# A linear-attention and SwiGLU kernel: earlier DMA transposes and loads, dummy matmuls in the opening, and other PSUM banks for the early state

## The chip, the cores and the metric

The kernel runs on one core of a Trainium2 chip. The metric is device microseconds (us) from the first to the last instruction of one execution, plus about 1.8 us of overhead. Each run carries a state: slow when it is over 1.5% above the fastest run of its kernel, else fast. The medians given are over all runs.

TensorE (PE) does matrix products, VectorE (DVE), ScalarE (ACT) and GpSimd (POOL) do elementwise work, SyncE (SP) issues DMAs. GpSimd also issues DMAs here: all loads that convert float32 to bfloat16 (k and q but for the first block, the weights) and, from block 4 on, the loads of v. PSUM is the memory, in banks, that the matrix products are written to. PEld in the views is TensorE's weight load.

## The reference, cut to what matters

Decayed linear attention over 4 batches x 8 heads x 768 tokens x 64, in blocks with a running state, followed by a SwiGLU feed-forward network (FFN).

```python
for b in range(nb):                                   # per block
    intra = (q_b @ k_b.T * Dmask) @ v_b
    inter = (q_b * lam_pow) @ kv_state
    out_b = intra + inter
    kv_state = lam_block * kv_state + (k_b * rev_pow).T @ v_b
x = out.transpose(0, 2, 1, 3).reshape(3072, 512)      # tokens x 512
y = (silu(x @ w_gate) * (x @ w_val)) @ w_out          # 512 -> 1536 -> 512
```

The kernel uses blocks of 128 tokens, so there are N = 24 blocks (6 per batch, NB = 6).

## The kernel before

The program order is written by hand, and each engine executes its instructions in that order. A block n passes four stages: `load` (DMA), `transposes` (k and q need their head dimension on the partitions), `scores` (k times q) and `cluster` (output and state). Blocks 0 to 7 are transposed on TensorE. From block 8 on (`PE_T = 8`) SyncE issues a DMA transpose instead.

```python
    PE_T = 8
    TILES = [(0, 4), (4, 2), (6, 2)] + [(i, 4) for i in range(8, N, 4)]   # first block, blocks per FFN tile
    ld = ctx.enter_context(tc.tile_pool(name="ld", bufs=7))               # loaded k and q
    vpool = ctx.enter_context(tc.tile_pool(name="vpool", bufs=7))         # loaded v
    ...
    def transposes(n):
        t = apool.tile([128, 2, HP, BLK], BF16, name="qkT", tag="qkT", bufs=4)
        if n >= PE_T:
            nc.sync.dma_start_transpose(out=..., in_=...)     # kq_nat -> qkT
        else:
            ...                                               # 8 TensorE transposes, copied out by ACT and DVE
    def scores(n):
        sp = ps_s.tile([128, 2, HP, BLK], FP32, name="sp", tag="sp")
        ...  nc.tensor.matmul(sp[:, h2, p, :], kT[n][r, p, :], qT[n][r, p, :], start=True, stop=True)
    def cluster(n, scores_of=None):
        ...  # op = kv_bd x qT      (L221, needs the state)
        if scores_of is not None:
            scores(scores_of)                                 # L207, needs qkT of the NEXT block
        ...  # op += v_s x ssb (L227); x = op; up = k x v (L240); new state kv_st, kv_bd
```

After an opening (blocks 0 to 7 and the first two FFN tiles), the main loop makes one step per block. A step is three FFN groups (`ffn_fc`, gate and value products, L273), one attention block, and one output product (`ffn_out`, L297) whose store is issued on SyncE:

```python
            for pos in range(3):
                ffn_fc(tt, 3 * per + pos)
                if pos == 0:
                    ...
                    if n + 1 < N:
                        scale_v(n + 1)                # GpSimd
                        transposes(n + 1)             # SyncE: DMA transpose
                elif pos == 1:
                    cluster(n, n + 1 if n + 1 < N else None)
                elif pos == 2:
                    if n + 4 < N:
                        load(n + 4)                   # GpSimd: k, q, v
                    ffn_out(*outs.pop(0))             # ends with a store on SyncE
```

`keep_warm(times)` issues dummy 128x512 matmuls, whose result nobody reads.

## Time and profile before

| | before |
|---|---|
| median time, us | 295.75 (4 runs, 293.63 to 300.65) |
| profiled span, us | 294.3 |
| TensorE busy, us | 242.5 |
| TensorE idle in waits for DMA transposes, us | 39.6 in 14 waits |

From the page of the kernel before: the totals, then rows over 40 equal slices of the span. A digit is tenths busy (9 is 90% or more); PEclk is the granted TensorE clock, the share of full speed that the chip allows at that time, in tenths.

```profile
span 294.3 us, 4235 instructions
...
PE 242.5 (82%) x1677; PEld 128.1 (44%) x1677; DVE 104.9 (36%) x168; ACT 79.3 (27%) x152; POOL 112.6 (38%) x150
...
PE   8689996999095839958599696896688999999994
...
PEclk9859996899759859999689997999979999999998
DMA  9999999990918792277491879254902200000122
```

TensorE has holes all through the middle of the run, and the granted clock dips with them. No engine is full there. Only the DMA row is full, and only in the first nine slices (up to about 66 us). TensorE is 90% busy or more in five of these nine slices, so what bounds the opening can't be read from these rows; in the middle it is no engine.

The list of waits names the cause (engine, line, waited for; us in total, times, longest):

```profile
PE sp L207 <- DMA qkT<-kq_nat: 39.6, 14, 7.6
```

Two stretches of the timeline show how one such wait comes about (start, us, engine, line, operation; in brackets the idle time before it and what ended it):

```profile
123.72 0.33 SPq L301 DMA_DIRECT2D out_dram<-osb  x1
124.22 1.46 SPq L184 DMA_TRANSPOSE qkT<-kq_nat  x1
...
126.36 0.39 PE L221 MATMUL op<-qkT,kv_bd 128*128 128x128 bf16 x4
...
129.75 0.40 PE L207 MATMUL sp<-qkT 64*128 64x128 bf16 x8 [3.00 <-DMA qkT<-kq_nat]
...
143.40 0.61 PE L207 MATMUL sp<-qkT 64*128 64x128 bf16 x8 [4.68 <-DMA qkT<-kq_nat]
...
144.72 1.89 PE L273 MATMUL gp<-xT,wg 128*128 128x512 bf16 x4
```

The transpose is issued right behind the store of the output before it, at 124.22. TensorE wants the result about 2.5 us later, at about 126.7, and gets it at 129.75. After a wait of 3.00 us the scores still run at full rate (0.40 us for eight). After 4.68 us they take 0.61, and four gate matmuls take 1.89 us where 1.03 is usual. That agrees with the Trainium skill, "TensorE: Matmul & The Clock Gate", Part 1, which says that the array clock falls to half after an idle window of about 3.4 us.

How long a transpose takes depends on what else moves. From the chain of waits (start, us, what):

```profile
73.32 8.29 DMA qkT<-kq_nat
...
114.69 3.05 DMA qkT<-kq_nat
```

```profile
71.90 0.95 POOL L84 DMA_DIRECT2D kq_nat<-in_k_dram  x1
72.85 0.88 POOL L85 DMA_DIRECT2D kq_nat<-in_q_dram  x1
73.71 0.91 POOL L79 DMA_DIRECT2D v_raw<-in_v_dram  x1
```

The transpose of 8.29 us runs beside the three loads of a block. Around the one of 3.05 us GpSimd issued no load: it did nothing between 110 and 120 us.

### The profile page before, as it was taken

To read this page: it belongs to the slowest core of one execution; us is meant where nothing else is said; L and a number is where in the kernel's file an instruction comes from. 1 tells how busy PE (TensorE), PEld (TensorE's weight loads), DVE (VectorE), ACT (ScalarE), POOL (GpSimd) and SP (SyncE) were. 2 spreads that over 40 slices of the span, in tenths; PEclk is the share of its full clock that TensorE was granted. 3 is DMA by queue.
4 is the path that set the end of the run, shared out by engine and by line. 5 is a ranking of instruction groups with operands and counts; after the bars stand their busy time and mean duration, and the time that the engine had idled before them with its cause. 6 is when DMAs were issued, how large, how long until landed. Compare 5 with 4: busy or idle time off the path is not lost.

```text
span 294.3 us, 4235 instructions
## 1 busy us (share of the span) xinstructions
PE 242.5 (82%) x1677; PEld 128.1 (44%) x1677; DVE 104.9 (36%) x168; ACT 79.3 (27%) x152; POOL 112.6 (38%) x150
## 2 busy tenths in 40 slices
PE   8689996999095839958599696896688999999994
PEld 3455454877054523433244342443244444444441
DVE  3744452566032322442214333334134242222200
ACT  6635433462001202212021130230203223232321
POOL 6796699714242820607154282062430310000000
PEclk9859996899759859999689997999979999999998
DMA  9999999990918792277491879254902200000122
GB/s 130 197 150 193 215 219 201 209 104 0 141 10 137 97 119 71 19 126 95 47 133 19 135 102 115 71 66 79 136 7 75 71 36 2 36 36 36 38 94 84
DMA packets 83075, 28.32 MB, mean 96 GB/s; under 512 B 73072, under 2 KB 78704, under 8 KB 83056
## 3 DMA queue, kind: packets, MB, share of 16 engines
q0 software_dynamic: 56320, 16.00, 50.5%
q1 hardware_dynamic: 26736, 12.07, 18.7%
q8 instruction: 13, 0.21, 0.3%
q14 instruction: 6, 0.05, 0.1%
HBM read 28.32 MB, written 6.29 MB: 118 GB/s over the span
## 4 chain that ended last, share of the span: by engine, by line
PE 67%; DMA 25%; POOL 3%; DVE 1%; ACT 1%; issue 1%; SPq 0%; ACTq 0%; DVEq 0%; POOLq 0%
DMA qkT<-kq_nat 23%; PE yp L297 22%; PE gp L273 20%; PE vp L273 17%; PE op L227 3%; PE sp L207 3%; DMA v_raw<-in_v_dram 2%; POOL v_s L177 1%; PE up L240 1%; DVE ssb L213 1%; PE tp L193 1%; PE op L221 1%; ACT kv_bd L251 1%; POOL wg L103 1%; DVE h_sb L289 0%
## 5 line engine op out<-in xcount | busy, mean ns | idle before, releaser
L289 DVE TENSOR_TENSOR h_sb<-sil,vp 128x512 bf16<-128x512 bf16 (+1 forms) x84 | 51.1, 611 | 123.3 <-PE vp L273 110.2
L273 PE MATMUL gp<-xT,wg 128*128 128x512 bf16 (+3 forms) x344 | 82.3, 365 | 0.8 <-ACT xT L232 0.7
L273 PE MATMUL vp<-xT,wv 128*128 128x512 bf16 (+3 forms) x344 | 81.1, 361 | 0.0
L286 ACT ACTIVATE sil<-gp 128x512 bf16<-128x512 f32 (+1 forms) x84 | 44.7, 536 | 124.8 <-PE gp L273 124.7
L297 PE MATMUL yp<-wo,h_sb 128*128 128x512 bf16 x288 | 68.1, 390 | 0.0
L253 POOL CAST kv_bd<-kv_st 64x256 bf16<-64x256 f32 x26 | 10.3, 396 | 113.8 <-DVE kv_st L246 83.4
L273 PEld LDWEIGHTS <-wv 128*128 128x128 bf16 x344 | 35.1, 103 | 32.1 <-issue 3.4
L273 PEld LDWEIGHTS <-wg 128*128 128x128 bf16 x344 | 32.8, 102 | 30.3 <-issue 3.6
L297 PEld LDWEIGHTS <-h_sb 128*128 128x128 bf16 x288 | 29.3, 102 | 35.9 <-issue 4.3
L207 PE MATMUL sp<-qkT 64*128 64x128 bf16 x192 | 10.8, 240 | 40.2 <-DMA qkT<-kq_nat 39.6
L213 DVE TENSOR_TENSOR ssb<-sp,mask 128x1024 bf16<-128x1024 f32 (+1 forms) x28 | 29.6, 1068 | 39.3 <-PE sp L207 39.3
L300 ACT COPY osb<-yp 128x512 f32<-128x512 f32 x24 | 14.1, 586 | 69.7 <-PE yp L297 69.7
L177 POOL TENSOR_TENSOR v_s<-v_raw,rev 128x512 bf16<-128x512 f32 x24 | 25.8, 1075 | 5.7 <-DMA v_raw<-in_v_dram 3.1
L207 PEld LDWEIGHTS <-qkT 64*128 64x128 bf16 x192 | 6.3, 102 | 45.1 <-DMA qkT<-kq_nat 42.6
L84 POOL DMA_DIRECT2D kq_nat<-in_k_dram x23 | 21.6, 939 | 1.6 <-DMA wg<-in_moe_w_gate_dram 0.8
L85 POOL DMA_DIRECT2D kq_nat<-in_q_dram x23 | 20.4, 888 | 2.5 <-DMA wg<-in_moe_w_gate_dram 1.5
L79 POOL DMA_DIRECT2D v_raw<-in_v_dram x20 | 18.2, 911 | 0.7 <-DMA wv<-in_moe_w_val_dram 0.7
L227 PE MATMUL op<-ssb,v_s 128*64 128x128 bf16 x192 | 12.0, 258 | 2.4 <-POOL v_s L177 2.4
L234 DVE TENSOR_TENSOR xT<-op,qscale 128x512 bf16<-128x512 f32 x16 | 10.9, 681 | 0.0
L221 PE MATMUL op<-qkT,kv_bd 128*128 128x128 bf16 x80 | 8.5, 233 | 2.4 <-ACT kv_bd L251 2.4
L227 PEld LDWEIGHTS <-v_s 128*64 128x64 bf16 x192 | 7.4, 127 | 5.8 <-POOL v_s L177 3.1
L221 PEld LDWEIGHTS <-kv_bd 128*128 128x128 bf16 x80 | 6.4, 104 | 5.8 <-ACT kv_bd L251 2.8
(47 smaller groups left out, 89.5 us busy)
## 6 DMA issues: line engine op xcount, KB each, us to landing
out_dram<-osb SPq DMA_DIRECT2D x24, 256.0 KB, 2.2
v_raw<-in_v_dram POOLq DMA_DIRECT2D x20, 256.0 KB, 6.0
kq_nat<-in_k_dram POOLq DMA_DIRECT2D x23, 128.0 KB, 4.7
kq_nat<-in_q_dram POOLq DMA_DIRECT2D x23, 128.0 KB, 5.7
wo<-in_moe_w_out_dram POOLq DMA_DIRECT2D x4, 384.0 KB, 7.7
wg<-in_moe_w_gate_dram POOLq DMA_DIRECT2D x3, 384.0 KB, 8.0
wv<-in_moe_w_val_dram POOLq DMA_DIRECT2D x3, 384.0 KB, 9.2
v_raw<-in_v_dram SPq DMA_DIRECT2D x4, 256.0 KB, 6.7
```

Source lines behind the costliest of these rows:

```text
L79: eng.dma_start(out=v_raw[n], in_=v5[b, j])
L84: nc.gpsimd.dma_start(out=t[:, 0], in_=k5[b, j])
L85: nc.gpsimd.dma_start(out=t[:, 1], in_=q5[b, j])
L177: nc.gpsimd.tensor_tensor(out=t, in0=v_raw.pop(n), in1=bap(rev, [[1, H], [0, D]]), op=ALU.mult)
L207: nc.tensor.matmul(sp[:, h2, p, :], kT[n][r, p, :], qT[n][r, p, :], start=True, stop=True)
L213: nc.vector.tensor_tensor(out=s[:, :, ps], in0=sp[:, :, ps], in1=mask[:, :, ps], op=ALU.mult)
L221: nc.tensor.matmul(op[:, p, :], kv_bd[n % 2][:, p, :], qT[n][:, p, :], start=(p == 0), stop=False, skip_group_check=True)
L227: nc.tensor.matmul(op[64 * h2:64 * h2 + 64, p, :], v_s[n][:, 2 * p + h2, :], ssb[n][:, h2, p, :], start=(j == 0 and p == 0), stop=(p == HP ...
L273: nc.tensor.matmul(gv[tt, fc][i][:, lo:hi], w[c][:, mc, fs], xT[:, mc, t0 + lo:t0 + hi], start=(mc == 0), stop=(mc == MC - 1))
L286: nc.scalar.activation(sil[:, 0:nt], gv[tt, fc][0][:, 0:nt], AF.Silu)
L289: nc.vector.tensor_tensor(out=h_sb[tt][:, fc, 0:nt], in0=sil[:, 0:nt], in1=gv.pop((tt, fc))[1][:, 0:nt], op=ALU.mult)
L297: nc.tensor.matmul(op, h_sb[tt][:, fc, sub * 128:(sub + 1) * 128], wo_sb[c][:, f, :], start=(fc == 0), stop=(fc == FC - 1))
```

## The change

The intent: issue DMA transposes three blocks ahead and loads six ahead, so that a transpose has two more steps to land; keep the clock up in the opening with 19 more dummies; move cluster 5 in between FFN matmuls of the second tile; and let the state accumulators (`up`) of blocks 4 to 7 use the output PSUM banks, which are free then.

```diff
-    ld = ctx.enter_context(tc.tile_pool(name="ld", bufs=7))
-    vpool = ctx.enter_context(tc.tile_pool(name="vpool", bufs=7))
-    apool = ctx.enter_context(tc.tile_pool(name="apool", bufs=3))
+    ld = ctx.enter_context(tc.tile_pool(name="ld", bufs=10))
+    vpool = ctx.enter_context(tc.tile_pool(name="vpool", bufs=9))
+    apool = ctx.enter_context(tc.tile_pool(name="apool", bufs=4))
 ... load_kq(1) moved behind the causal mask; qkT bufs 4 -> 6
-            up = (ps_o if n < FIRST else ps_f).tile(...)
+            up = (ps_o if n < PE_T else ps_f).tile(...)
 ... opening:
     scores(0)
-    transposes(1)
     scale_v(1)
     load_w(0)
+    keep_warm(5)
     cluster(0)
+    transposes(1)
+    nc.scalar.activation(primed, lamb, AF.Silu)
+    keep_warm(2)
     scores(1)
 ... and so on for blocks 1 to 3: value scaling earlier, keep_warm(4), (1), (4), (3)
 ... end of the first tile and second tile:
-        elif fc == 10:
-            scale_v(5)
-            transposes(5)
-        elif fc == 11:
-            cluster(4, 5)
-            cluster(5)
+        elif fc == 9:
+            cluster(4)
+            transposes(5)
+        elif fc == 10:
+            scores(5)
+            load(8)
+    fc_mms(1, 0, 0, BLK)
+    cluster(5)
+    fc_mms(1, 1, 0, BLK)
+    ffn_fc(1, 0, BLK)
+    ffn_fc(1, 1, BLK)
 ... loads 9 to 13 and the DMA transposes 8 to 10 inside the second tile
 ... main loop:
                         scale_v(n + 1)
-                        transposes(n + 1)
+                    if n + 3 < N:
+                        transposes(n + 3)
-                    if n + 4 < N:
-                        load(n + 4)
+                    if n + 6 < N:
+                        load(n + 6)
```

## The prediction

> **What bounds the kernel now.** Span 294.3 us, TensorE busy 242.5. By the list of waits, TensorE stood idle 39.6 us in 14 waits of score matmuls for a DMA transpose (longest 7.6 us); the chain of waits puts 23% of the span on those transposes. The timeline shows why: each transpose is issued 3 to 4 us before its scores and takes 3.0 to 8.3 us to land. The longer waits cost twice: after them matmuls run at half rate for 3 to 4 us (four 512-wide gate matmuls take 1.82 us instead of 0.86), which agrees with the Trainium skill, "TensorE: Matmul & The Clock Gate", Part 1: the clock halves after an idle window of about 3.4 us. So the main loop is bound by transpose latency, not by an engine. In the opening (to 65 us) the DMA engines are 90% busy or more in nearly every slice, at about 200 GB/s, and weight pieces land only 1 to 3 us before use.
>
> **What the change does.**
> 1. Transposes go out three blocks ahead (17 us more lead), loads six ahead; no work is added. This should remove all of the 39.6 us and the half clock behind it. A step without waits, by the last steps of the timeline: three fc groups of 1.73, one output of 2.59, attention matmuls of about 1.0: 8.7 us. From the third tile on: 4 short steps x 6.2 = 25; 12 steps = 104; 4 steps without attention x 7.77 = 31; last outputs 10.4; tail 4: 174 us, against 229 before (65 to 294). Saving 55: 40 idle, about 12 half clock.
> 2. Cluster 5 moves behind fc work of the second tile. Before, clusters 4 and 5 back to back cost about 3 us idle (44.1 to 48.4), then half clock until 53: about 6 us saved. The split 128-wide matmuls cost nothing (four take 0.22 us, 256-wide 0.44).
> 3. 19 more dummies, 4.1 us at full clock, fill waits of the opening and keep the clock up where it was 0.5 to 0.6 (12 to 22 us). But the first tile then meets weights that land 1 to 3 us before use, and two pieces are issued 1.1 us later. I expect -1.5 to +2 us.
> 4. Early state accumulators move from the FFN's PSUM banks to output banks idle then: about 0.
> 5. Two more blocks load in the opening: 1.5 MB, about 7.5 us at 200 GB/s, while TensorE arrives 6 us earlier. The first one or two transposes of the main loop may still be late: 2 to 4 us lost.
>
> **Sum.** Third tile starts at about 59, plus 174, plus 3 late: span 236, time about 238 us. Range 231 to 249. Faster by over 2%: 0.97; within: 0.02; slower: 0.01.
>
> **What would show it.** Step 1: waits for transposes fall from 40 to under 4 us, clock 1.0 in almost all slices after 70 us, step 8.7 us. Step 2: no gap and no half clock at 44 to 53 us. Step 3: clock near 1.0 from 12 to 22 us, second tile within 2 us of before. Step 5: a last transpose wait at 59 to 70 us at most.
>
> **What would make it wrong.** GpSimd (5.2 us of issue, scaling and casts per 8.7 us step) held up by full DMA queues; VectorE chains that the stalls hid; transposes slower under denser traffic; a clock throttled under unbroken matmul load (the last 50 us ran unbroken at 1.0, so I doubt it); a first tile waiting for weights.

## The result and the profile after

The changed kernel takes 245.93 us (median of 4 runs, 243.27 to 247.67) against 295.75. The ratio is 0.8305, with a 95% interval of 0.8203 to 0.8408. A ratio is the mean time of one kernel's fast runs over that of the other's of the same rounds, so it is not quite the ratio of the medians. The time lies inside the predicted range (231 to 249), 8 us above the predicted 238.

The same rows of the page after:

```profile
span 244.4 us, 4264 instructions
...
PE 227.9 (93%) x1687; PEld 121.8 (50%) x1712; DVE 105.3 (43%) x168; ACT 79.5 (33%) x152; POOL 111.8 (46%) x150
...
PE   7688999998379999999999999999999999999993
...
PEclk9999999999979999999999999999999999999999
DMA  7999999999999999999799993513101110111022
```

TensorE is full from the thirteenth slice on, at full clock. One hole is left, at about 61 to 69 us, with a clock dip behind it. The list of waits has two waits for transposes where there were 14:

```profile
PE sp L207 <- DMA qkT<-kq_nat: 5.1, 2, 2.9
```

TensorE's timeline shows both, and what they cost afterwards:

```profile
60.84 0.60 PE L273 MATMUL gp<-xT,wg 128*128 128x256 bf16 x4
...
64.04 0.40 PE L207 MATMUL sp<-qkT 64*128 64x128 bf16 x8 [2.16 <-DMA qkT<-kq_nat]
...
68.59 0.40 PE L207 MATMUL sp<-qkT 64*128 64x128 bf16 x8 [2.95 <-DMA qkT<-kq_nat]
...
69.94 1.06 PE L273 MATMUL vp<-xT,wv 128*128 128x256 bf16 x4
```

The scores of blocks 8 and 9, the first two that need DMA transposes, are late. The value matmuls at 69.94 take 1.06 us instead of 0.60: half clock. The 5.1 us of waits are more than the "under 4 us" of the prediction's list of signs. From about 75 us on this view shows no further wait of TensorE. The start times of the output products give the step of the main loop:

```profile
99.51 2.75 PE L297 MATMUL yp<-wo,h_sb 128*128 128x512 bf16 x12
108.41 2.75 PE L297 MATMUL yp<-wo,h_sb 128*128 128x512 bf16 x12
117.30 2.75 PE L297 MATMUL yp<-wo,h_sb 128*128 128x512 bf16 x12
```

A step is 8.9 us.

### The profile page after: what moved, and what is told of

It is laid out like the page before. It is cut to its first block, busy times and chain, and to the rows that moved or that the text cites. A ratio compares the mean times of both kernels' runs of the same rounds, so it can differ in the third digit from the quotient of the medians.

```text
span 244.4 us, 4264 instructions
## 1 busy us (share of the span) xinstructions
PE 227.9 (93%) x1687; PEld 121.8 (50%) x1712; DVE 105.3 (43%) x168; ACT 79.5 (33%) x152; POOL 111.8 (46%) x150
## 4 chain that ended last, share of the span: by engine, by line
PE 85%; DMA 8%; ACT 2%; issue 1%; DVE 1%; SPq 1%; POOL 0%; ACTq 0%; POOLq 0%
PE yp L297 26%; PE gp L273 25%; PE vp L273 24%; DMA qkT<-kq_nat 5%; PE op L227 3%; PE sp L207 3%; DMA v_raw<-in_v_dram 3%; PE op L221 2%; PE tp L193 1%; PE up L240 1%; ACT xT L232 1%; ACT kv_bd L251 1%; ACT qkT L195 0%; POOL v_s L177 0%; PE warm_ps L126 0%
## 5 line engine op out<-in xcount | busy, mean ns | idle before, releaser
L273 PE MATMUL gp<-xT,wg 128*128 128x512 bf16 (+3 forms) x336 | 75.9, 340 | 1.5 <-ACT sil L286 0.6
L273 PE MATMUL vp<-xT,wv 128*128 128x512 bf16 (+3 forms) x352 | 77.1, 342 | 0.1
L297 PE MATMUL yp<-wo,h_sb 128*128 128x512 bf16 x281 | 65.5, 383 | 0.5 <-issue 0.2
L273 PEld LDWEIGHTS <-wv 128*128 128x128 bf16 x352 | 33.9, 98 | 29.1
L273 PEld LDWEIGHTS <-wg 128*128 128x128 bf16 x352 | 31.6, 98 | 28.1 <-issue 1.0
L253 POOL CAST kv_bd<-kv_st 64x256 bf16<-64x256 f32 x26 | 10.2, 392 | 64.1 <-DVE kv_st L246 47.9
L207 PE MATMUL sp<-qkT 64*128 64x128 bf16 x192 | 9.5, 218 | 7.4 <-DMA qkT<-kq_nat 5.1
L227 PE MATMUL op<-ssb,v_s 128*64 128x128 bf16 x192 | 10.1, 225 | 1.4 <-POOL v_s L177 1.2
L126 PE MATMUL warm_ps<-warm 128*128 128x512 bf16 x30 | 9.6, 452 | 1.4 <-DVE warm L121 1.2
L227 PEld LDWEIGHTS <-v_s 128*64 128x64 bf16 x192 | 6.1, 109 | 4.4 <-POOL v_s L177 1.6
L232 ACT CAST xT<-op 128x512 bf16<-128x512 f32 x8 | 4.7, 585 | 10.4 <-PE op L227 10.4
```

What stands on the lines that cost most here:

```text
L227: nc.tensor.matmul(op[64 * h2:64 * h2 + 64, p, :], v_s[n][:, 2 * p + h2, :], ssb[n][:, h2, p, :], start=(j == 0 and p == 0), stop=(p == HP ...
L273: nc.tensor.matmul(gv[tt, fc][i][:, lo:hi], w[c][:, mc, fs], xT[:, mc, t0 + lo:t0 + hi], start=(mc == 0), stop=(mc == MC - 1))
L297: nc.tensor.matmul(op, h_sb[tt][:, fc, sub * 128:(sub + 1) * 128], wo_sb[c][:, f, :], start=(fc == 0), stop=(fc == FC - 1))
```

## The experiments

All kernels gave correct results. Times are medians. "Fast mean" is the mean of the fast runs, which the ratios use. Ratios are to the kernel before. The experiments were made in three groups of rounds on different chips, and the fast mean of the kernel before was 294.7, 297.0 and 296.3 us in them, so times of different groups are comparable to about 1%.

### 1. Which part is the gain?

**Only the lead of the transposes, on the kernel before.**

```diff
-        t = apool.tile(..., name="qkT", tag="qkT", bufs=4)
+        t = apool.tile(..., name="qkT", tag="qkT", bufs=6)
             scale_v(8)
             transposes(8)
+            transposes(9)
+            transposes(10)
 ... main loop:
-                        transposes(n + 1)
+                    if n + 3 < N:
+                        transposes(n + 3)
```

> The kernel before with one part of the change: transposes three blocks ahead instead of one (and six transposed tiles instead of four); loads stay four ahead, seven load buffers, old opening, old second tile, no more dummies. Theory A (the lead of the transposes is nearly all of it): waits of TensorE for transposes from 40 us to under 6, time 241 to 250 us. Rival B (loads six ahead are needed, because a transpose waits for its source to land): most of the 40 us stays, time above 265 us.

Measured: 246.03 us, ratio 0.8335 (0.8236 to 0.8434). One wait of TensorE's matmuls for a transpose is left, and the page gives the busy times:

```profile
68.28 0.40 PE L207 MATMUL sp<-qkT 64*128 64x128 bf16 x8 [3.82 <-DMA qkT<-kq_nat]
```

```profile
PE 228.5 (93%) x1677; PEld 122.1 (50%) x1677; DVE 103.3 (42%) x168; ACT 79.2 (32%) x152; POOL 112.4 (46%) x150
```

So a few changed lines give the whole gain, with no more loads, buffers for loads, dummies or moved clusters. The trace of this kernel has the same number of matmul records as the one before (1677), so the difference in TensorE's busy time, 242.5 - 228.5 = 14.0 us, is clock. The waits for transposes fell by 39.6 - 3.8 = 35.8 us. Together that is 49.8 us, and the spans differ by 49.7 (294.3 - 244.6).

**All of the change but the lead.** In the changed kernel the transposes go back to one block ahead.

```diff
-            transposes(9)
             load(13)
-    transposes(10)
 ... main loop:
-                    if n + 3 < N:
-                        transposes(n + 3)
+                    if n + 1 < N:
+                        transposes(n + 1)
```

> The changed kernel with only the transposes put back to one block ahead; loads six ahead, dummies, moved cluster and PSUM banks stay. Theory A: the waits for transposes come back (35 to 45 us idle and half clock behind them), time 280 to 292 us, so that the rest of the change is worth 4 to 15 us at most. Rival B: the loads six ahead are the gain, time under 262 us.

Measured: 292.97 us, ratio to the kernel before 0.9956 (0.9858 to 1.0053), which is not distinguishable from it. It waits like the kernel before:

```profile
PE sp L207 <- DMA qkT<-kq_nat: 38.3, 16, 5.3
```

Rival B falls in both runs: loading six ahead is neither needed nor enough. Nor are the two more transposed tiles, which this kernel has too. (The time is 1 us above the range that I had written down.)

**Is a lead of two enough?**

```diff
-                    if n + 3 < N:
-                        transposes(n + 3)
+                    if n + 2 < N:
+                        transposes(n + 2)
 ... and transposes(10) dropped before the loop
```

> The changed kernel with the transposes two blocks ahead instead of three. Theory A: a lead of one step more (over 8 us) already covers the 3 to 8 us of a transpose in the main loop; the same waits as in the changed kernel at 62 to 69 us, time 244 to 248 us. If three blocks are needed: waits for transposes of over 10 us in sum, time above 252 us.

Measured: 251.07 us (249.34 to 252.65), 5 us above the changed kernel; the profiled runs differ by 3.2 us (spans 247.6 and 244.4). Neither expectation fits. This profile's opening ran 2 us late (its first 512-wide gate matmul starts at 27.10 us, not at 25.06), but that did not carry on: the scores of blocks 9, 10 and 11 start 1.5 to 1.6 us before those of the changed kernel (67.08, 74.97 and 81.31 us against 68.59, 76.60 and 82.94). The loss comes in the next short step of the third tile, at block 12:

```profile
90.83 0.43 PE L207 MATMUL sp<-qkT 64*128 64x128 bf16 x8 [3.12 <-DMA qkT<-kq_nat]
```

That transpose was issued at 80.6 us, beside loads, and took 10.2 us to land. The scores of block 12 are then 1.6 us behind the changed kernel's, and those of block 13 3.1 us behind (100.10 against 96.97), as the span is at the end. So my figure of 3 to 8 us was too small for this kernel. In the main loop, a lead of two brought one wait back; a lead of three has none there.

That a kernel runs without stalls does not by itself make its transposes slow: it depends on whether they meet loads. Four transposes of the main loop, first with only the lead (105 to 134 us), then in the changed kernel (102 to 134 us):

```profile
L184 SPq DMA_TRANSPOSE qkT<-kq_nat x4: 1239/1484/1889, 107.0 to 133.6; - x4
...
DMA to landing us min/median/max: 3.0/3.1/3.2
```

```profile
L184 SPq DMA_TRANSPOSE qkT<-kq_nat x4: 1459/1492/2010, 103.4 to 130.1; - x4
...
DMA to landing us min/median/max: 5.9/6.2/6.5
```

Neither kernel stalls there. With loads four ahead, a transpose is issued about 3 us after the last load's issue (115.71 after 111.83), with loads six ahead in the middle of the loads (112.31, loads issued from 110.12 to 111.92). The deeper loads made these transposes slower, and the lead hides it.

### 2. What is left in the changed kernel, at 62 to 69 us?

**The changed kernel without its 19 dummies.**

```diff
-    keep_warm(5)
     cluster(0)
 ... and the five others: (2), (4), (1), (4), (3)
```

> The changed kernel without its 19 new dummy matmuls. Theory A: the granted clock between 12 and 22 us falls back to 0.5 to 0.7, but everything before about 69 us is held by the first two transposes of the main loop (their data comes when the DMA queues let it), so the time stays within 1 us of the changed kernel's 246 us. Rival C (the warm opening is carried to the end): 2 to 4 us longer, 248 to 250 us.

Measured: 246.32 us (fast mean 246.5, against 245.0 for the changed kernel in other rounds), too close to tell apart. The dummies do what they are for. The view by windows shows it, first of the changed kernel, then of this one. Its columns are the stretch, its length, the busy us (and instructions) of PE, PEld, DVE, ACT and POOL, the granted clock, a DMA share and GB/s:

```profile
12.00:16.00 4.00, 3.05 (x49) 2.04 (x49) 2.64 (x7) 3.57 (x7) 4.00 (x6) 1.00 1.63 152
16.00:20.00 4.00, 3.00 (x38) 1.76 (x35) 2.90 (x6) 2.54 (x6) 3.99 (x6) 1.00 1.15 131
```

```profile
12.00:16.00 4.00, 3.32 (x44) 2.57 (x44) 2.36 (x6) 3.21 (x6) 4.00 (x5) 0.50 1.82 174
16.00:20.00 4.00, 2.39 (x28) 1.87 (x28) 2.69 (x6) 2.48 (x6) 4.00 (x6) 0.50 1.17 145
```

TensorE is busy a similar time in both, but its clock is 1.00 with the dummies and 0.50 without. (They do not always suffice: in the profile with a lead of two, which has them, it was 0.57 from 12 to 16 us.)

The scores of block 9, however, start at 68.59 us in the changed kernel, at 68.28 with the old opening (experiment "only the lead"), and at 67.92 without the dummies. Whatever the opening gains, the transpose of block 9 arrives at about 68 us. How much the dummies gain in the opening, single profiles don't settle. Without them the first 512-wide gate matmul starts at 26.80 us, with them at 25.06, and in the kernel before, with its other order of the opening and no new dummies, at 24.67. But in the profiles of other kernels here with the same opening and dummies it starts anywhere from 24.42 to 27.10 us.

**Earlier data for blocks 8 and 9.** The four output-weight loads go behind the loads of blocks 8 and 9.

```diff
         elif fc == 7: ...
-            for c in range(2):
-                load_wo(c)
+            load(8)
         elif fc == 8: ...
-            for c in range(2, 4):
-                load_wo(c)
+            load(9)
         elif fc == 10:
             scores(5)
-            load(8)
+            for c in range(4):
+                load_wo(c)
```

> The changed kernel with the four output-weight loads (1.5 MB in SBUF, 3.1 MB read) moved behind the loads of blocks 8 and 9, so that these two blocks and their transposes come earlier. Theory A: the two waits of 2.2 and 2.9 us for transposes at 62 to 69 us, and the half clock after them, vanish or shrink to under 1 us; time 237 to 241 us, if the output weights still land before 67 us. Rival D (a transpose among heavy loads takes over 10 us whenever it is issued, and four issued in a row hold one another up): a wait of 2 us or more for a transpose stays, time 243 us or more.

Measured: 248.26 us, probably slower than the changed kernel (fast mean 248.5 against 245.0; the intervals of the ratios, 0.8326 to 0.8505 here, overlap). The transposes of blocks 8 and 9 are issued about 7 us earlier, at 46.0 and 49.1 instead of 53.3 and 55.9 us, but take 12.3 and 16.8 us to land instead of 10.6 and 12.6 (from the transposed tile's view of 46 to 58 us):

```profile
L184 SPq DMA_TRANSPOSE qkT<-kq_nat x2: 1486/2755/4024, 46.0 to 49.1; - x2
...
DMA to landing us min/median/max: 12.3/14.5/16.8
```

Block 8 is then in time, block 9 still late, and block 10 is late as well:

```profile
65.95 0.40 PE L207 MATMUL sp<-qkT 64*128 64x128 bf16 x8 [2.50 <-DMA qkT<-kq_nat]
...
78.16 0.61 PE L207 MATMUL sp<-qkT 64*128 64x128 bf16 x8 [4.20 <-DMA qkT<-kq_nat]
```

The k and q of block 10 were loaded from 51.3 us on, at nearly the same time as in the changed kernel (50.9), but behind the output weights they took 15.3 us to land instead of 6.4. So the transpose of block 10 was issued at 67.7 us instead of 59.1, and its wait is the longer of the two.

The DMA view of 46 to 58 us, in 40 slices of 0.3 us, shows the transfer rate while both run beside the output weights:

```profile
DMA  9999999989993799999999999999999998999997
GB/s 149 106 73 81 134 207 262 349 211 189 125 65 51 39 73 81 76 79 83 74 80 71 83 86 107 110 69 75 82 82 78 86 87 132 202 194 171 152 143 120
```

The engines are busy, but move only about 80 GB/s for some 6 us (49 to 56 us), where the opening otherwise moves about 200. Theory A's cure was wrong: it took away one wait of two and made a longer one. The first half of rival D held here: each of the transposes among heavy loads took over 10 us (12.3, 16.8 and 10.5). That four in a row hold one another up was not shown.

**Fewer loads beside these transposes.** The loads of blocks 10 to 13 wait behind the scaling of v of block 9, which waits for its data and so starts at 56.79 us.

```diff
             scale_v(7)
+            scale_v(8)
+            scale_v(9)
             load(10)
 ...
             load(11)
-            scale_v(8)
 ... main loop: scale_v(n + 1) only from block 10 on
```

> The changed kernel with the loads of blocks 10 to 13 held back on GpSimd until the values of block 9 are scaled (about 58 us instead of 51 us), so that the transposes of blocks 8 and 9 run among fewer loads. Theory E (a DMA transpose among software-queued loads takes 10 us and more instead of 3, and this is what makes the first scores late): the transposes of blocks 8 and 9 land within 3 to 7 us, no wait of over 1 us for them; then either a new short wait for block 10 or none; time 238 to 243 us. Rival F (all data of the opening is moved by the same engines, so that holding loads back only moves the lateness to block 10 or 11): waits for transposes of 4 us or more in sum stay, time 244 us or more.

Measured: 240.45 us, ratio 0.8088 (0.801 to 0.8166). The landing times of the transposes of blocks 8 and 9, first in the changed kernel, then here:

```profile
L184 SPq DMA_TRANSPOSE qkT<-kq_nat x2: 1334/2160/2985, 53.3 to 55.9; - x2
...
DMA to landing us min/median/max: 10.6/11.6/12.6
```

```profile
L184 SPq DMA_TRANSPOSE qkT<-kq_nat x2: 1334/1678/2023, 53.5 to 55.9; - x2
...
DMA to landing us min/median/max: 3.9/4.7/5.5
```

The same two transposes, issued at the same times, land in less than half the time when no further loads are issued beside them. TensorE then waits 0.32 us for a transpose in the whole run. The only edit is the order of loads and scalings on GpSimd, so theory E is shown: the lateness was made by the loads queued beside the transposes. It agrees with the Trainium skill, "DMA: Bandwidth & Descriptors", section "Queues, rings and completion order": each DMA engine goes round the queues that have work, a packet at a time, so a transpose shares the engines with whatever loads are queued.

**No DMA transposes there at all.** Blocks 8 and 9 are transposed on TensorE.

```diff
+    TP = 10
-        if n >= PE_T:                        # in transposes; the same in the copy of x
+        if n >= TP:
 ... transposes(8) after FFN group 10 of the second tile, transposes(9) after group 11, transposes(10) after group 9
```

> The changed kernel with blocks 8 and 9 transposed on TensorE (16 more matmuls, about 0.9 us) instead of by DMA. Theory E: no wait for transposes at 62 to 69 us, no half clock after them, 5.1 + 2.3 us saved less 0.9: time 238 to 241 us. Rival F: the loads themselves are what is late, so a wait for the loads of blocks 8 or 9, or for the transpose of block 10, of 3 us or more takes its place; 243 us or more.

Measured: 240.26 us, ratio 0.8108 (0.8036 to 0.8181), and no wait for a transpose. The same edit with the old opening, on "only the lead":

```diff
 ... the kernel of "only the lead of the transposes", with TP = 10 as above
```

> The kernel before with the lead of three blocks alone (as in the first experiment) and blocks 8 and 9 transposed on TensorE: old opening, old second tile, no new dummies. If the gain of the new opening was hidden behind the late transposes in the changed kernel (theory A), this is 1.5 to 6 us slower than the changed kernel with the same blocks on TensorE. If the new opening gives nothing even where nothing hides it, both are within 1 us.

Measured: 244.55 us (fast mean 244.3, against 240.8 for the one above in the same rounds). So where late transposes no longer hide it, the rest of the change (new opening, second tile, loads six ahead, PSUM banks) is together worth about 3.5 us, from four runs each; the intervals of the ratios overlap (0.8121 to 0.8303 here). In the changed kernel it was worth nothing that could be measured.

### 3. The small parts, one by one, where nothing hides them

Three parts were undone, each alone, on the kernel with held-back loads, five rounds each, in one group with that kernel again as control.

> The kernel with the loads held back (unchanged from that experiment), as the control of this group, because the next three each undo one part of the change on it. No theory is tested; it should give 239 to 242 us again.

```diff
 ... no edit: the held-back loads again, as the control
```

Measured: 241.1 us (240.15 to 241.13), fast mean 240.9, ratio 0.8133 (0.8108 to 0.8158). Its profile has two small waits at block 10, so that holding the loads back moved a little of the lateness on, as rival F said:

```profile
69.67 0.40 PE L221 MATMUL op<-qkT,kv_bd 128*128 128x128 bf16 x4 [1.05 <-POOL kv_bd L253]
...
70.52 0.40 PE L207 MATMUL sp<-qkT 64*128 64x128 bf16 x8 [0.45 <-DMA qkT<-kq_nat]
```

> The control without the 19 new dummy matmuls. Theory A (their gain was hidden behind the late transposes in the changed kernel and shows where those are on time): 1 to 3 us above the control, the half clock between 12 and 22 us back, no new wait. Rival G (the first tile waits for its weights or for the other engines anyway): within 0.7 us of the control.

```diff
-    keep_warm(5)
     cluster(0)
 ... and the five others, as before
```

Measured: 241.5 us, fast mean 241.5, 0.6 us above the control; the ratio is 0.8148 (0.8124 to 0.8172) and the intervals overlap, but all six runs (241.14 to 242.03) lie above the control's six, so a small gain of the dummies is likely. By the numbers written down, this is rival G's side, but its reason is not shown. In the profiles the first 512-wide gate matmul starts 2.8 us later than in the control (27.22 against 24.42 us), with half clock between 12 and 24 us, and this kernel then has neither of the control's two waits at block 10. So a later start of TensorE seems to have been given back there; as said above, this start varies by 2.7 us between profiles with the dummies too.

> The control with the state accumulators of blocks 4 to 7 back in the FFN's PSUM banks. Prediction, step 4: within 0.7 us of the control. Rival: the FFN matmuls of the second tile wait for a bank, 1 us or more above the control.

```diff
-            up = (ps_o if n < PE_T else ps_f).tile(...)
+            up = (ps_o if n < FIRST else ps_f).tile(...)
```

Measured: 240.77 us, fast mean 240.9 like the control. The PSUM banks are worth nothing measurable here.

> The control with cluster 5 put back directly behind cluster 4 at the end of the first tile. Prediction, step 2: the idle of about 2.1 + 0.7 us for the state and for xT comes back at 44 to 49 us, and in the runs in which the clock then falls, up to 3 us more: 2.5 to 6 us above the control. Rival: the other engines' work placed there hides it, under 1.5 us.

```diff
-        elif fc == 9:
-            cluster(4)
+        elif fc == 10:
             transposes(5)
-        elif fc == 10:
-            scores(5)
             load(8)
+        elif fc == 11:
+            cluster(4, 5)
+            cluster(5)
 ... and the second tile starts with ffn_fc(1, 0) and ffn_fc(1, 1)
```

Measured: 242.93 us, fast mean 242.9, 1.9 us above the control; the ratio is 0.8193 (0.8167 to 0.8219), clear of the control's interval. The idle time came back as predicted, and in this profile the clock fell with it (0.60 granted between 48 and 52 us):

```profile
47.36 0.40 PE L221 MATMUL op<-qkT,kv_bd 128*128 128x128 bf16 x4 [2.14 <-ACT kv_bd L251]
48.94 1.01 PE L273 MATMUL gp<-xT,wg 128*128 128x256 bf16 x4 [0.68 <-ACT xT L232]
```

The effect is below the 2.5 to 6 us that I had written down. This kernel, too, has no wait at block 10, so part of the loss may have been regained there.

## Why the prediction was right, point by point

The reading was right: the kernel before was bound by the latency of DMA transposes, a longer lead removes it, and the time fell in the predicted range. The best estimate was 8 us too low. The predicted span of 236 us splits against the measured 244.4 as follows.

| term | predicted, us | measured, us | from |
|---|---|---|---|
| start of the third tile | 59 | 60.8 | its first gate matmul in the timeline after |
| from there to the end, without waits | 174 | 177 | held-back loads: 237.9 - 60.3 - 0.5 of waits |
| late first transposes | 3 | 6.6 | 244.4 - 60.8 - 177 |

- **Step 1 (lead).** Right, and shown alone: the lead by itself gives 246.03 us. The saving was 49 to 50 us instead of 55. Idle and clock were sized well (35.8 and 14.0 us, predicted 40 and 12). The step without waits was mis-sized: 8.9 us, not 8.7, which over 12 steps is 2.4 us of the 3 that the second row is off.
- **Step 2 (cluster 5).** Right in mechanism. It removed 2.1 + 0.7 us of idle and the half clock behind it. Predicted 6 us; undone where late transposes did not hide it, 1.9 us at the end. In the changed kernel it was not undone alone.
- **Step 3 (dummies).** The expected -1.5 to +2 us holds (0.6 us where nothing hid it). The granted clock did stay at 1.0 in the profile after. The reason that I gave, weights that land late, was not seen: TensorE's waits in the profile after name no weight load. What was seen is that later transposes swallow the gain.
- **Step 4 (PSUM banks).** About 0, as predicted.
- **Step 5 (late first transposes).** The place was right, the size too small (6.6 instead of 3 us: 5.1 idle, the rest, by subtraction, mostly half clock), and the cause was only half right. I blamed two more blocks of data. "Only the lead" loads no such blocks in the opening and still waits 3.82 us. What delays the transposes is the loads queued beside them: with these held back, the same transposes land in 3.9 and 5.5 us instead of 12.6 and 10.6.
- **What would make it wrong.** I listed transposes slower under denser traffic. That happened: with a lead of two blocks, one took 10.2 us and TensorE waited for it, and in the changed kernel those issued between 66 and 147 us took 5.5 to 11.0 us, against 3.0 to 6.0 with only the lead.

What stays open: why the DMA engines at times move so much less while transposes run beside loads. In the run with the late output weights it was about 80 GB/s for some 6 us, but in the changed kernel the rate stayed at 198 to 236 GB/s from 52 to 58 us and fell to 111 and 46 only from 58 to 62 us.

The best kernels, the held-back loads and the two blocks transposed on TensorE, take 240.5 and 240.3 us, against 245.9 for the change and about 296 for the kernel before.

## What to carry to other kernels

When an engine waits again and again for a short transfer, issue the transfer earlier before anything else: the order of a few lines gave all of the 50 us here, and deeper load buffers, dummies and moved work gave nothing measurable beside it. Size the lead by how long the transfer takes beside the traffic of the kernel as it will be, not of the stalled one, and keep bulk loads away from a transfer that something waits for. An improvement ahead of a late transfer is hidden until that transfer comes on time, so mend the last wait first and measure the others after it.

## What the Trainium skill lacked or had wrong

- "DMA: Bandwidth & Descriptors", section "DMA Transpose (X-bar)", gives no time for a transpose between SBUF tiles beside other transfers. Here one of a block's k and q took 3.0 us without loads issued around it, 8.3 us beside one block's loads, 10.6 and 12.6 us beside more, and 12.3 and 16.8 us beside the output weights, where the rate was about 80 GB/s for some 6 us.
- "TensorE: Matmul & The Clock Gate", Part 1, gives an idle window of about 3.4 us. Single waits agree in part: 3.00 us left the clock full and 4.68 halved it, but after one of 3.18 us (lead put back to one; a wait of 1.79 us lay 5 us before it) eight scores took 0.61 us, so half clock. The clock can also fall after the wait has ended: after waits of 2.95 us (the changed kernel, with one of 2.16 us some 4 us before it) and 3.82 us (only the lead) eight scores still took 0.40 us, and FFN matmuls about 1 us later ran at half rate (1.06 and 1.02 us instead of 0.60). Two shorter gaps of 2.14 and 0.68 us in a row halved it in the kernel before and left it full in "only the lead". The page does say that the window runs freely and that results vary from run to run.
- The same Part says that the clock rises after a busy window of about 3.4 us. In the opening without dummies it stayed at 0.50 from 12 to 20 us, while TensorE was busy 3.32 and 2.39 of 4 us with small matmuls and transposes. How much of a window must be busy, the page does not say.
